# Output stores moved from GpSimd's queue to SyncE's queue in a forward-and-backward joint-network kernel

## The chip, the cores and the metric

The kernel runs on one core of a Trainium2 chip. Its engines are TensorE (PE, with its weight loads shown apart as PEld), VectorE (DVE), ScalarE (ACT), GpSimd (POOL) and SyncE (SP). The transfers between memory and the on-chip buffers are made by 16 DMA engines, which all issuing engines share. The metric is device time of the core in microseconds (us), the median of several runs. The profile is one execution, taken by the hardware profiler.

## The reference

The forward pass takes x (2 batches, 16000 steps, 256 channels). A convolution of width 3 with weights w1 is followed by gelu and by dropping every second step; the same again with w2. The 4000 steps that remain in each batch go through w_f and are joined with each of 8 label rows of g (through w_g) by a sum and a tanh; w_o gives the output, 2 x 4000 x 8 x 256. Then the gradients of all seven inputs are formed from grad_out, which has the output's shape. All data are bfloat16.

```python
def _fwd_reference(x, w1, w2, g, w_f, w_g, w_o):
    h = zeros;  for i in range(3): h = h + einsum("btc,cd->btd", xp[:, i:i+T, :], w1[i])
    h = _gelu(h)[:, ::2, :]
    f = zeros;  for i in range(3): f = f + einsum("btc,cd->btd", hp[:, i:i+T1, :], w2[i])
    f = _gelu(f)[:, ::2, :]
    fe = jnp.einsum("btd,de->bte", f, w_f)
    ge = jnp.einsum("bud,de->bue", g, w_g)
    j = jnp.tanh(fe[:, :, None, :] + ge[:, None, :, :])
    return jnp.einsum("btud,dv->btuv", j, w_o)

_out, _vjp = jax.vjp(_f, x, w1, w2, g, w_f, w_g, w_o)
_grads = _vjp(grad_out)
```

## The kernel before

**Tiling.** The 4000 remaining steps of a batch are cut into nine chunks: one of 256, seven of 512 and one of 160 in the first batch; seven of 512, one of 256 and one of 160 in the second. That makes 18 chunks. The loop at the end of the kernel (lines 973 to 1000) goes over them as a software pipeline. While chunk k is in its joint stage (`stage_j`), the forward convolutions of chunk k+1 (`stage_a`) and the backward pass of chunk k-1 (`stage_de`) run in between.

**What is moved, and by whom.** SP issues:

- XC (x transposed, one buffer of this class) for the convolutions, from `load_xc`;
- GOT (grad_out transposed, 8 buffers), one transfer per chunk and label, from `load_got`;
- GO_R (grad_out in rows, 6 buffers), 2 labels by up to 256 steps, from `load_gor`;
- X5 (x in rows, 4 buffers), one transfer per block of 128 steps, from `load_x5`;
- HRo, HRs, HRe and FR (rows of the activations, made by transposing transfers from one on-chip tile to another), from `dma_rows`;
- at the end, the weight gradients out of the g_sq tiles (two buffers).

POOL issues the two large outputs: out (OUT_SB, 6 buffers, stored in `stage_j`, lines 676 to 688) and the gradient of x (GX_SB, 3 buffers, stored in `stage_de`, lines 841 to 853). A pair of labels and half a chunk (256 steps) fill one OUT_SB; PE's results are copied into it by ACT or DVE (line 674), two blocks of 128 steps one after the other. A block of 128 steps of the gradient of x fills one GX_SB. POOL also copies the one-column halos between chunks and clears pads.

**First and last blocks.** At the first block of a batch the first of its four phases falls outside of x, so that X5 and GX_SB are moved as 1 row and then 127 rows; at the batch's last block a few rows are left. All other blocks are moved with 128 rows.

**What sets the order.** Nothing is issued as the code is read. Every operation is recorded by `F.op` with an estimated cost, its reads and writes, the buffers it opens and a due time. Then `Flow.issue` (lines 104 to 191) runs through a model of the machine: at each step it takes the operation that can start first, among equals the one due first, and writes it to its engine's instruction list. So a change in the model's times changes the order of all lists. Each engine then executes its list in order, and waits for the semaphores of what it depends on. The lines of the model that matter here:

```python
if o.work:                                   # a transfer (line 128)
    ln = lanes[e == "POOL"]
    if len(ln) >= 8:
        s = max(s, ln[-8] + wake)
...
o.done = ring[e] + 2000.0 + self.MARGIN      # line 174; MARGIN is 6500 ns
lanes[e == "POOL"].append(o.done - 1.0 * self.MARGIN)
```

A transfer is believed complete at `done`, and a buffer that it reads is believed free from then. The list `lanes` holds when recent transfers are believed to be over, apart for POOL and for the others: a transfer may not start before the eighth before it in the same list. In the model a store on POOL costs 750 ns of issue for out and 550 for the gradient of x, a plain transfer on SP 400 and a transposing one 1260 (line 332). In the built program eight semaphores in turn serve the transfers of SP and another eight those of POOL, and each transfer waits for the one that had its semaphore before.

Of the kernel before, what the change touches and what calls it, by code (L numbers as in the profile page):

```python
# [17 lines left out]
GELU_A = float(2.0 * np.sqrt(2.0 / np.pi))  # L18


LOADQ, STOREQ = "SP", "POOL"
HR_AT = (0.7, 0.4, 0.3)
A_AT = (0.1, 0.25, 0.4, 0.6)

# [16 lines left out]
class Flow:  # L41
# [62 lines left out]
    def issue(self):  # L104
        T = {e: 0.0 for e in self.WAKE}
        avail = {e: [] for e in T}
        ring = {"SP": 0.0, "POOL": 0.0, "ACT": 0.0}
        lanes = {True: [], False: []}
        left, prog = len(self.ops), -1e12
        slots, seq = self.slots, self.seq  # L110

        def put(o):
            o.ready = max((d.done for d in o.deps), default=0.0)
            for e in o.eng:
                avail[e].append(o)

        for o in self.ops:
            if o.left == 0:
                put(o)
        while left:  # L120
            best = None
            for e, lst in avail.items():
                t, wake, cand = T[e], self.WAKE[e], None
                for o in lst:
                    if o.nb is not None and prog < o.nb:
                        continue
                    s = o.ready + wake
                    if o.work:
# [3 lines that stand above are left out]
                    for b in o.new:  # L132
                        st = seq[b.cls]
                        if not st[2] and st[1] != b.seq:
                            s = None
                            break
                        f = min((x[1] for x in slots[b.cls] if x[1] is not None), default=None)
                        if f is None:
                            s = None
                            break  # L140
                        s = max(s, f + wake)
                    if s is None:
                        continue
                    k = (max(s, t), o.prio, o, e)
                    if cand is None or k < cand:
                        cand = k
                if cand is not None and (best is None or cand[0] < best[0]):
                    best = cand
            if best is None:
                prog = min((o.nb for lst in avail.values() for o in lst if o.nb is not None and o.nb > prog), default=None)  # L150
                assert prog is not None, "no operation can start"
                continue
            s, _, o, e = best
            if o.lead:
                prog = max(prog, o.prio[0])
            for x in o.eng:
                avail[x].remove(o)
            for b in o.new:
                free = [i for i, x in enumerate(slots[b.cls]) if x[1] is not None]
                i = min(free, key=lambda i: (slots[b.cls][i][1], i))  # L160
                b.slot, slots[b.cls][i][1] = i, None
                seq[b.cls][1] += 1
                b.t = slots[b.cls][i][0].tile(b.shape, b.dtype, name=b.name, tag=b.cls)
            T[e] = s + o.cost[o.eng.index(e)]
            if o.work:
                a = max(ring[e], T[e] - 400.0)
                if e == "POOL":
                    ring[e] = a + o.work
                    for q in ("SP", "ACT"):
                        if ring[q] > a:  # L170
                            ring[q] += o.work
                else:
                    ring[e] = max(a, ring["POOL"]) + o.work
                o.done = ring[e] + 2000.0 + self.MARGIN
                lanes[e == "POOL"].append(o.done - 1.0 * self.MARGIN)
            else:
                o.done = T[e] + self.TAIL[e]
            o.inst = o.fn(e)
            for h in o.hold:
                self.tc.add_manual_dep(o.inst.ins, h.inst.ins.name, mybir.DependencyInfo(  # L180
                    mybir.DependencyClass.Sync, mybir.DependencyReason.DATA), reason="order of the first loads")
            left -= 1
            for b in o.bufs:
                b.users -= 1
                if b.users == 0 and b.cls is not None:
                    slots[b.cls][b.slot][1] = o.done
            for d in o.succ:
                d.left -= 1
                if d.left == 0:
                    put(d)  # L190
        self.T = T
# [838 lines left out]
```

## Time and profile before

| | |
|---|---|
| median of 3 runs | 841.24 us (841.03 to 841.38) |
| profiled execution | 841.38 us |
| span of the profiled execution | 839.6 us |
| PE busy | 803.0 us, 96% |
| DVE, ACT busy | 763.0 us, 749.2 us |
| POOL busy | 185.3 us, 22% |
| POOL's stores of out, issue | 136 (95.5 us) |
| POOL's stores of the gradient of x | 68, median 0.56 us each |
| DMA queue of SP (q1) | 120.54 MB, 71.0% of 16 engines |
| DMA queue of POOL (q0) | 49.98 MB, 18.9% of 16 engines |

A row of a timeline gives the start in us from the span's start, the duration, the engine, the line, the operation and its tiles. "SPq" is SP's issuing of a transfer; the duration is that of issuing, with any wait inside it, and the landing of the data comes later. "X" in the profile is X5, "XC" the transposed x; buffer numbers are left out. A DMA view gives the bytes moved in 40 equal slices of its window, in GB/s, and then the transfers issued in the window with the median time from issue to landing, where it could be matched.

### The profile page before, as it was taken

How to read it: one execution, taken by the hardware profiler on the slowest of the kernel's cores; microseconds unless marked ns; L12 is line 12 of the kernel's file. 1: busy time of each engine (PE TensorE's matmuls, PEld its weight loads, DVE VectorE, ACT ScalarE, POOL GpSimd, SP SyncE). 2: the span in 40 equal slices, each digit the busy share in tenths (PEclk: the TensorE clock that was granted, in tenths of full speed). 3: DMA queues.
4: the chain of work that ended last, by engine and by line, in shares of the span. 5: the costliest groups of instructions: out<-in, count | busy, mean ns of one | idle time of the engine just before them, and what ended most of it. 6: DMA issues, size and time to landing. Idle time of an engine off the chain costs nothing.

```text
span 839.6 us, 18037 instructions
## 1 busy us (share of the span) xinstructions
PE 803.0 (96%) x6428; PEld 595.5 (71%) x6428; DVE 763.0 (91%) x1731; ACT 749.2 (89%) x1206; POOL 185.3 (22%) x391
## 2 busy tenths in 40 slices
PE   7479999999999999999999999999999999999994
PEld 5346767677686767877777677676776868788983
DVE  4679999998999989998989999998989999998992
ACT  5859999999899998988899999998898989988762
POOL 2101221212122111223131303121121212123241
PEclk9889999999999999999999999999999999999998
DMA  9989999999989896987988999999899896958442
GB/s 181 128 158 237 198 224 240 262 244 228 226 207 241 200 254 153 219 224 196 187 189 118 245 223 264 241 209 267 220 222 229 212 247 166 255 154 200 125 138 67
DMA packets 330594, 172.06 MB, mean 205 GB/s; under 512 B 275142, under 2 KB 310250, under 8 KB 330504
## 3 DMA queue, kind: packets, MB, share of 16 engines
q1 hardware_dynamic: 313944, 120.54, 71.0%
q0 software_dynamic: 15776, 49.98, 18.9%
q8 instruction: 50, 0.82, 0.4%
q10 hardware_dynamic: 784, 0.39, 0.2%
q14 instruction: 40, 0.33, 0.1%
HBM read 54.44 MB, written 50.34 MB: 125 GB/s over the span
## 4 chain that ended last, share of the span: by engine, by line
PE 72%; DVE 11%; ACT 7%; DMA 3%; issue 3%; SPq 2%; POOL 0%; DVEq 0%; ACTq 0%; POOLq 0%
PE ps L306 58%; PE GWO L306 10%; PE psb L483 4%; SPq L329 2%; DVE NGZ L651 2%; DVE ZS L659 2%; DMA GOT<-in_grad_out_dram 2%; ACT g_sq L432 1%; DVE g_s L436 1%; ACT JT L589 1%; ACT JR L609 1%; ACT JSQ L641 1%; ACT OUT_SB L314 1%; DVE JR L602 1%; DMA out_dram<-g_sq 1%
## 5 line engine op out<-in xcount | busy, mean ns | idle before, releaser
L589 ACT ACTIVATE JT<-FE,GE 128x512 bf16<-128x512 bf16 (+2 forms) x288 | 187.7, 689 | 0.7 <-DVE FE L319 0.7
L331 POOL DMA_DIRECT2D out_dram<-OUT_SB x136 | 95.5, 702 | 361.8 <-ACT OUT_SB L314 242.0
L306 PE MATMUL ps<-GOT,WT 128*128 128x512 bf16 (+2 forms) x576 | 154.8, 354 | 13.1 <-DMA GOT<-in_grad_out_dram 12.8
L651 DVE SCALAR_TENSOR_TENSOR NGZ<-JSQ,ps 128x512 f32<-128x512 bf16 (+2 forms) x252 | 152.1, 606 | 14.6 <-PE ps L306 14.5
L306 PE MATMUL ps<-WO,JT 128*128 128x256 bf16 x1024 | 153.9, 273 | 1.6 <-ACT JT L589 1.0
L609 ACT ACTIVATE JR<-JR 128x1024 bf16<-128x1024 bf16 x128 | 138.2, 1085 | 4.2 <-DVE JR L602 3.9
L641 ACT ACTIVATE JSQ<-JT 128x1024 bf16<-128x1024 bf16 (+2 forms) x119 | 117.5, 990 | 24.1 <-DVE NGZ L651 24.0
L306 PEld LDWEIGHTS <-JT 128*128 128x128 bf16 x1024 | 99.6, 98 | 54.8 <-ACT JT L589 1.8
L306 PE MATMUL GWO<-GO_R,JR 128*128 128x256 bf16 x1024 | 133.6, 274 | 1.1 <-ACT JR L609 1.1
L314 ACT CAST OUT_SB<-ps 128x512 bf16<-128x512 f32 x205 | 125.5, 613 | 9.6 <-PE ps L306 9.6
L659 DVE TENSOR_TENSOR ZS<-ZS,NGZ 128x512 f32<-128x512 f32 (+2 forms) x216 | 131.1, 610 | 0.2
L306 PEld LDWEIGHTS <-WT 128*128 128x128 bf16 x864 | 81.7, 98 | 49.1 <-DMA GOT<-in_grad_out_dram 13.1
L306 PEld LDWEIGHTS <-JR 128*128 128x128 bf16 x1028 | 100.3, 98 | 19.9 <-ACT JR L609 2.7
L306 PEld LDWEIGHTS <-W 128*128 128x128 bf16 x648 | 61.8, 99 | 58.0 <-issue 3.7
L306 PE MATMUL ps<-XC,W 128*128 128x512 bf16 (+2 forms) x432 | 93.5, 355 | 0.8 <-DVE NGZ L651 0.8
L306 PE MATMUL ps<-ROWS,X 128*128 128x256 bf16 x768 | 92.0, 273 | 0.0
L602 DVE TENSOR_TENSOR JR<-FER,GEB 128x1024 bf16<-128x1024 bf16 x128 | 87.2, 683 | 1.0 <-PE GWO L306 1.0
L306 PEld LDWEIGHTS <-X 128*128 128x128 bf16 x768 | 75.1, 98 | 9.1
L436 DVE SCALAR_TENSOR_TENSOR g_s<-g_sq,ps 128x512 bf16<-128x512 bf16 (+2 forms) x108 | 65.9, 611 | 15.8 <-ACT HTo L434 12.6
L707 DVE TENSOR_TENSOR ACC<-ACC,ps 128x512 f32<-128x512 f32 x96 | 64.1, 678 | 11.5 <-PE ps L306 11.3
L432 ACT ACTIVATE g_sq<-ps 128x512 bf16<-128x512 f32 (+2 forms) x108 | 60.4, 559 | 15.3 <-PE ps L306 12.7
L306 PE MATMUL ps<-WT,GHe 128*128 128x256 bf16 x384 | 73.3, 273 | 0.7 <-ACT ROWS L314 0.7
(135 smaller groups left out, 1264.0 us busy)
## 6 DMA issues: line engine op xcount, KB each, us to landing
GO_R<-in_grad_out_dram SPq DMA_DIRECT2D x120, 256.0 KB, 3.9
out_dram<-OUT_SB POOLq DMA_DIRECT2D x120, 256.0 KB, 4.4
X<-in_x_dram SPq DMA_DIRECT2D x60, 320.0 KB, 5.5
out_dram<-GX_SB POOLq DMA_DIRECT2D x60, 256.0 KB, 4.1
GOT<-in_grad_out_dram SPq DMA_TRANSPOSE x144, 4.7
out_dram<-g_sq SPq DMA_DIRECT2D x9, 128.0 KB, 1.8
GO_R<-in_grad_out_dram SPq DMA_DIRECT2D x8, 128.0 KB, 3.1
out_dram<-OUT_SB POOLq DMA_DIRECT2D x8, 128.0 KB, 3.2
```

The costliest lines, as they stand in the source:

```text
L306: nc.tensor.matmul(ps_ap, lhsT=lhsT, rhs=rhs, start=start, stop=stop)
L314: nc.scalar.copy(out=dst(), in_=src())
L331: return eng_.dma_start(out=out(), in_=in_())
L432: op("ACT", c_act(W, True), lambda e, mt=mt, ps=ps: nc.scalar.activation(out=sq[:, mt, :W], in_=ps[:, :W], func=ACT.Square, scale=GELU_SQR ...
L436: op("DVE", c_dve(W), lambda e, mt=mt, ps=ps: nc.vector.scalar_tensor_tensor(out=s[:, mt, :W], in0=sq[:, mt, :W], scalar=1.0, in1=ps[:, :W ...
L589: op("ACT", c_act(W, ptr=True), lambda e, j=j, mt=mt: nc.scalar.activation(out=JT[:, j, mt, :W], in_=S["FE"][:, mt, :W], func=ACT.Tanh, bi ...
L602: op("DVE", c_dve(n * 2 * D, 0.5), lambda e, lo=lo, n=n, m=m, JR=JR: nc.vector.tensor_tensor(out=JR[:m, lo % 2:lo % 2 + n], in0=S["FER"][: ...
L609: op("ACT", c_act(n * 2 * D), lambda e, lo=lo, n=n, m=m, JR=JR: nc.scalar.activation(out=JR[:m, lo % 2:lo % 2 + n], in_=JR[:m, lo % 2:lo % ...
L641: nc.scalar.activation(out=JSQ[:, :, :W], in_=JT[:, j, :, :W], func=ACT.Square)
L651: op("DVE", c_dve(W) + 6, lambda e, d2=d2, ps=ps, u=u, zap=zap, JSQ=JSQ: nc.vector.scalar_tensor_tensor(out=zap(), in0=JSQ[:, d2, :W], sca ...
L659: op("DVE", c_dve(W), lambda e, d2=d2, dst=dst, NGZ=NGZ: nc.vector.tensor_tensor(out=dst[:, d2, :W], in0=ZS[:, d2, :W], in1=NGZ[:, :W], op ...
L707: op("DVE", c_dve(512), lambda e: nc.vector.tensor_tensor(out=acc_ap().rearrange("p k d -> p (k d)"), in0=acc_ap().rearrange("p k d -> p ( ...
```

## The change

The queue of the steady stores becomes SP in place of POOL. All transfers in the steady state are then issued by SP, in one list. And in the planner's model of the limit of eight transfers in flight, a transfer is believed over 0.6 x 6.5 us = 3.9 us before its believed completion, in place of 6.5 us.

```diff
-LOADQ, STOREQ = "SP", "POOL"
+LOADQ, STOREQ = "SP", "SP"
...
                 o.done = ring[e] + 2000.0 + self.MARGIN
-                lanes[e == "POOL"].append(o.done - 1.0 * self.MARGIN)
+                lanes[e == "POOL"].append(o.done - 0.6 * self.MARGIN)
```

A store on SP costs 400 ns of issue in the model (line 332). The stores that use `STOREQ` are those of out and of the gradient of x, 204 in number; the small outputs at the end and the loads of the weights stay where they were.

## The prediction

> **What bounds the kernel now.** I read the page's busy shares first, then busy time by stretch of the span, then the stage in which the changed queue has least room.
>
> The page, section 1, and the slices of section 2:
>
> ```profile
> PE 803.0 (96%) x6428; PEld 595.5 (71%) x6428; DVE 763.0 (91%) x1731; ACT 749.2 (89%) x1206; POOL 185.3 (22%) x391
> ...
> PE   7479999999999999999999999999999999999994
> ```
>
> Busy time in three stretches; the columns are PE, PEld, DVE, ACT, POOL, granted clock, DMA share, GB/s:
>
> ```profile
> 0.00:63.00 63.00, 42.17 (x287) 27.22 (x287) 37.25 (x112) 39.48 (x74) 10.24 (x28) 0.86 0.91 156
> 63.00:798.00 735.00, 730.75 (x5847) 542.54 (x5848) 701.04 (x1542) 691.65 (x1097) 162.82 (x335) 1.00 0.94 215
> 798.00:839.60 41.60, 30.03 (x297) 25.69 (x294) 24.69 (x79) 18.09 (x37) 12.24 (x28) 0.95 0.33 104
> ```
>
> TensorE is the bound. From 63 to 798 us it idles 735.0 - 730.8 = 4.2 us at the full clock, so nothing there can be gained, and any wait that reaches PE is added to the end. The start loses 20.8 us and the end 11.6. The question is whether the reordered SP queue can keep PE's inputs and, above all, the output buffers coming.
>
> How the trace prices a transfer over 127 rows: load_x5 has two such loads (the first block of each batch), on SP already. SP's own issue rows, then the DMA view of 439 to 455 us (40 slices of 0.4 us):
>
> ```profile
> 437.41 1.96 SPq L331 DMA_DIRECT2D X<-in_x_dram  x5
> 439.47 14.71 SPq L329 DMA_TRANSPOSE GOT<-in_grad_out_dram  x1
> 454.27 0.53 SPq L331 DMA_DIRECT2D GO_R<-in_grad_out_dram  x1
> ```
>
> ```profile
> GB/s 436 182 192 155 183 239 312 284 191 70 29 26 26 26 26 26 323 333 36 26 26 26 51 155 193 35 19 26 26 26 26 26 26 29 27 23 26 26 26 26
> ...
> X<-in_x_dram SPq DMA_DIRECT2D x1, 317.5 KB
> ```
>
> After the 317.5 KB load the core moves 26 GB/s, a tenth of its usual rate: one DMA engine works and 15 rest, for 325,120 B / 26 GB/s = 12.5 us. SP's next transpose takes 14.7 us to issue instead of the median 1.28. The same load sits in the start: 26 GB/s from 34 to 42 us, and PE's longest wait (12.8 us, for GOT) ends behind it.
>
> The store with the same 127 rows is on POOL today, and lands like any other:
>
> ```profile
> out_dram<-GX_SB POOLq DMA_DIRECT2D x1, 254.0 KB, 3.6
> ```
>
> Who needs the queue at that time: POOL issued that store at 95, SP was issuing without a pause up to 124, and ACT's copy into the 15th output buffer came at 118.7:
>
> ```profile
> 95.17 1.07 POOL L331 DMA_DIRECT2D out_dram<-GX_SB  x2 [1.32 <-ACT GX_SB L316]
> ```
>
> ```profile
> 116.60 2.55 SPq L329 DMA_TRANSPOSE FR<-FT  x2
> 119.24 0.53 SPq L331 DMA_DIRECT2D GO_R<-in_grad_out_dram  x1
> 119.83 4.02 SPq L329 DMA_TRANSPOSE GOT<-in_grad_out_dram  x3
> ```
>
> ```profile
> 118.69 0.67 ACT L314 CAST OUT_SB<-ps 128x512 bf16<-128x512 f32 x1
> ```
>
> **What the skill says.** The Trainium skill, "DMA: Bandwidth & Descriptors", section "Why a DMA increments its semaphore by 16 and not by 1": a hardware-generated transfer is spread over the largest k up to 16 that divides the slowest dimensions, so 127 partitions go to one engine, the lowest-numbered, while the software path from POOL uses 16 engines for 127. The trace agrees on both: 26 GB/s for the load on SP, 3.6 us to landing for the 254 KB store on POOL. Same page, "Queues, rings and completion order": each engine consumes a queue's ring in order and takes turns between queues. So a 16-way transfer behind a 127-row one in SP's ring has one sixteenth of itself waiting; the 14.7 us row fits. Same page, "SWDGE vs HWDGE vs iDMA": DVE can lock POOL out while it writes descriptors in SBUF, and the hardware path is free of that. No row shows that lockout costing PE anything.
>
> **The change part by part.** Removed: 204 of POOL's steady stores (136 of OUT_SB, mean 702 ns, 95.5 us; 68 of GX_SB, 0.56 us, 38 us). Worth 0: POOL is 22% busy and none of PE's longer waits names it.
>
> Added: the same 204 on SP. Priced as its loads of the same shape (GO_R 0.53, X 0.44 us): 136 x 0.53 + 68 x 0.44 = 102 us. SP now issues some 144 x 1.28 + 144 x 1.25 + 32 x 3.1 + 136 x 0.53 + 68 x 0.44 = 565 us; it gets 667, 79% of the span. Hidden in steady state behind SP's waits for slots (223 us on PE at the transposes alone). Behind each store in SP's order stand the loads, which now wait for its copy by ACT or DVE. GOT (8 buffers) and GO_R (6) are fetched tens of us ahead, so a few us cost nothing. In the built program each SP transfer also waits for the eighth before it; stores now share these eight with loads. At 738 transfers per 840 us and 4 to 5 us to landing, four or five are in flight: binds only behind a long one.
>
> Planner line 175: believed completions in the eight-transfer limit come 0.4 x 6.5 us later. No instruction is added; the order moves. PE's list is identical for 288 matmuls, which is up to 63 us, then permuted. GX_SB's slots are planned with the same distance as before. 0, -1 to +3.
>
> Start: POOL's output stores of 32.4 and 35.9 us took 10.5 us to land, beside the 127-row load. They now come after PE's long wait: two sixteenths of 256 KB leave that engine, 2 x 16 KB / 26 GB/s = 1.2 us. Estimate -1 (0 to -2.5).
>
> First 127-row store (GX_SB of the first chunk). Its issue: before, SP issues 41 transfers from 63.7 to 119.8. In the new order the store comes after the same list without one GOT (1.3), one GO_R (0.6) and two X (1.6), with eight stores at 0.6, and one store earlier (0.6): 56.1 - 3.5 + 4.8 + 0.6 = 58.0, so at 121.7, less 1 from the start: 120.7. It moves 260,096 B at 26 GB/s, 10.0 us, and some 3 us of fixed landing time (3.6 minus 0.6 transfer on POOL): 133.7. Directly behind it stands the store of the 9th output buffer: 134. With six buffers the 15th takes the slot of the 9th, and ACT's copy into it waits for this landing. ACT gets there at 118.7 - 1 = 117.7, and stands 16 us, with tanh, squares and PSUM copies queued behind it. PE goes on until its seven PSUM banks are full, at 0.43 us for two 512-column matmuls some 2 to 3 us. Cost 14 us (9 to 20; below if it issues earlier, above if the next stores, held by SP's blocked transpose, come late too).
>
> Second 127-row store (first chunk of batch two): POOL issued it at 508.4, and the fourth GX_SB block, which takes its slot, was copied at 520.3. From SP at 509 or later it lands at 522: 2 us late, more by SP's backlog (up to 10). Take +3 (0 to 12). Tail: the output chain (g_sq stores, 1.85 us each) stays on SP; the last GX_SB stores are ready before it: 0, +-1.
>
> Sum: -1 + 14 + 3 + 1 (scattered late slots) = +17. The profiled execution is 841.38 us, 1.78 around its span of 839.6; the median of the runs is 841.24, 0.14 less. So span 856.6, time 858.4, for the median 858.
>
> **Rivals.** (1) The store spreads over 16 engines from SP too, or the buffers absorb it. For: PE has been full through the SP hold-up of 439 to 454. Against: the slot is needed 16 us before landing. Then only the eight extra issues count: the store of the 7th buffer issues near 102 and lands at 106.6, against a copy at 106.1. +2 to +6: 845. (2) SP becomes the bound. For: its transposes took 1.25 to 2.4 us each between 85 and 104, with a DMA share of 1.04. At 1.7 each, 288 x 0.45 = 130 us more: 667 + 130 + two holds of 13 = 823 of 840, and late slots recur in every chunk: +35 to +60, 885. Against: 1.25 us is common from 110 on. (3) Faster: the start gains its 1 to 2.5 us and both 127-row stores hide: 839.5. It decides if the first issues before about 105, so that it lands by 118.7. For that SP would have to shed 16 us of its list; against, it is continuously issuing there. (4) No change: a loss of 1 in slots against the start, 841.
>
> **How the numbers follow.** Main case 0.66, its own range 850 to 872 (parts: start -2.5 to 0, first store 9 to 20, second 0 to 12). Rival 1: 0.13; 2: 0.10; 3: 0.06; 4: 0.05. The range 842 to 880 leaves rivals 3 and 4 (0.11) below, and most of 2 (0.08) above. A difference under 0.2% (1.7 us) can't be told from none: faster 0.06, same 0.05, slower 0.89.
>
> **What would show it.** Right: 26 GB/s for some 10 us from about 121, an SP transpose issue over 8 us there, ACT idle before an OUT_SB copy on DMA, PE idle 9 to 20 us in one gap between 115 and 140, a small one near 520, and 4 us elsewhere. PE's first 63 us shorter by 1. Wrong: GX_SB's 254 KB store landing in 4 to 5 us from SP; PE gaps spread evenly over chunks (SP the bound); a PE busy time that itself grew.

## The result and the profile after

The changed kernel takes 870.3 us (median of 6 runs, 868.11 to 872.49) against 841.31 us of the kernel before beside it (6 runs): a ratio of 1.034, 95% interval 1.0317 to 1.0362, or 29.0 us more. The profiled execution has a span of 866.9 us, 27.3 more than before.

The page of the changed kernel, busy shares and the slices of PE and of its clock:

```profile
PE 809.1 (93%) x6428; PEld 597.5 (69%) x6428; DVE 763.2 (88%) x1733; ACT 747.7 (86%) x1204; POOL 57.1 (7%) x187
...
PE   8489959999999999999999996799999999999994
...
PEclk9799989999999999999999999899999999999998
```

POOL is freed of 128 us of work, and nobody gains by it. PE has the same 6428 matmuls, is busy 6.1 us longer, and shows two new dents: a 5 in the sixth slice (108 to 130 us), and a 6 and a 7 from 520 to 563 us, each time with a lower clock.

Busy time in the same three stretches as before (stretch, length, then PE, PEld, DVE, ACT, POOL, granted clock, DMA share, GB/s):

```profile
0.00:63.00 63.00, 45.61 (x309) 30.02 (x310) 40.29 (x119) 42.22 (x78) 7.27 (x24) 0.89 0.82 151
63.00:800.00 737.00, 708.24 (x5579) 519.33 (x5578) 673.34 (x1459) 668.44 (x1055) 41.92 (x140) 0.99 0.93 209
800.00:867.00 67.00, 55.26 (x544) 48.20 (x542) 49.56 (x157) 37.01 (x73) 7.92 (x23) 0.95 0.42 128
```

In the middle PE idled 4.2 us before; now it idles 737.0 - 708.2 = 28.8 us. The start lost 3.4 us of idling (17.4 for 20.8). The end is as it was (11.7 for 11.6).

PE's waits, costliest first (total us, times, longest us):

```profile
PE ps L306 <- ACT ROWS L314: 12.2, 3, 10.5
PE ps L306 <- ACT GX_SB L316: 11.9, 2, 11.2
PE ps L306 <- DMA GOT<-in_grad_out_dram: 10.5, 1, 10.5
```

The third is the start's wait, 12.8 us before. The first two are new, and each is one long gap. The span's growth thus adds up: -3.4 (start) + 10.5 (first gap) + 11.2 (second) + 2.8 (the rest of the middle: 24.5 - 21.7) + 0.1 (end) + 6.1 (PE busy longer) = 27.3 us.

**The first gap.** The chain that ended last, 113 to 135 us:

```profile
113.92 12.62 DMA out_dram<-OUT_SB
126.62 0.35 ACT OUT_SB L314
...
127.11 1.03 ACT ROWS L314
128.17 6.41 PE ps L306 x28
```

SP's issues there, and the bytes moved from 100 to 140 us (40 slices of 1 us):

```profile
113.14 0.68 SPq L331 DMA_DIRECT2D out_dram<-GX_SB  x2
113.92 3.26 SPq L331 DMA_DIRECT2D out_dram<-OUT_SB  x1
117.23 5.93 SPq L329 DMA_TRANSPOSE GOT<-in_grad_out_dram  x1
```

```profile
GB/s 170 311 369 288 231 10 130 131 58 296 144 89 69 132 8 14 20 82 159 168 68 25 27 25 27 25 186 312 378 295 377 302 245 293 6 273 380 305 412 368
```

The store of 127 rows goes out at 113.5 as the second of the pair; its data had been copied by 91.5. Directly behind it stands a full-width store of out, which lands 12.6 us after its own issue; only then may ACT copy into that buffer. The five slices at 25 to 27 GB/s from 121 to 126 us fit the one-engine store alone on the queue: from 121.2 to 125.8 us the 16 DMA engines are busy 0.07 of the time, and one of 16 is 0.0625.

**The second gap** has the same face, with the buffer of the gradient of x itself (chain, then SP):

```profile
532.11 13.13 DMA out_dram<-GX_SB
545.35 0.60 ACT GX_SB L316
```

```profile
531.78 4.70 SPq L331 DMA_DIRECT2D out_dram<-GX_SB  x3
536.58 4.14 SPq L329 DMA_TRANSPOSE GOT<-in_grad_out_dram  x1
```

The data of that store was ready much earlier. A GX_SB block takes two copies; ACT's first begins at 516.72 and the second ends near 519.2. The store is issued at 532, nearly 13 us later. (POOL, before, issued it 1.2 us after its second copy.)

**PE's clock after a gap.** Stretches of 4 us (length, PE busy, granted clock, DMA share, GB/s):

```profile
126.00:130.00 4.00, 1.83 (x9) 0.50 1.05 293
130.00:134.00 4.00, 4.00 (x20) 0.63 1.57 304
134.00:138.00 4.00, 4.00 (x29) 1.00 0.87 241
545.00:549.00 4.00, 3.00 (x8) 0.50 1.13 181
549.00:553.00 4.00, 4.00 (x25) 0.95 0.94 158
```

After the first gap PE comes back at half its clock at 128.2 us: its first eight 256-column matmuls take 1.86 us, where eight such take 1.04 before the gap. If the clock is either half or whole, a mean of 0.63 means half speed for 3.0 of the 4 us, so the slow spell lasts about 5 us. After the second gap, from 546.0, it lasts about 3.4 us by the same reckoning. The Trainium skill, "TensorE: Matmul & The Clock Gate", section "Part 1: The HAM clock gate (the "warmup" mystery)", gives the array these two rates: an idle window of some 3.4 us drops it to half, and about 3.4 us of sustained work releases it. The trace agrees after the second gap; after the first the slow spell is longer.

Half speed takes 0.50 x 1.83 + 0.37 x 4.00 = 2.4 us from PE after the first gap and 0.50 x 3.00 + 0.05 x 4.00 = 1.7 us after the second. That is at most 4.1 of the 6.1 us by which PE is busy longer; where the rest comes from was not found.

### The profile page after: what moved, and what is told of

It is laid out like the page before. It is cut to its first block, busy times and chain, and to the rows that moved or that the text cites. A ratio compares the mean times of both kernels' runs of the same rounds, so it can differ in the third digit from the quotient of the medians.

```text
span 866.9 us, 17921 instructions
## 1 busy us (share of the span) xinstructions
PE 809.1 (93%) x6428; PEld 597.5 (69%) x6428; DVE 763.2 (88%) x1733; ACT 747.7 (86%) x1204; POOL 57.1 (7%) x187
## 4 chain that ended last, share of the span: by engine, by line
PE 64%; DVE 13%; ACT 13%; DMA 6%; issue 2%; SPq 0%; DVEq 0%; ACTq 0%; POOL 0%
PE ps L306 52%; PE GWO L306 9%; PE psb L483 3%; ACT JT L589 3%; DVE NGZ L651 2%; ACT JR L609 2%; DVE g_s L436 2%; DVE ZS L659 2%; DMA out_dram<-GX_SB 2%; ACT g_sq L432 1%; DMA out_dram<-OUT_SB 1%; DMA GOT<-in_grad_out_dram 1%; ACT OUT_SB L314 1%; ACT JSQ L641 1%; DVE GHo L763 1%
## 5 line engine op out<-in xcount | busy, mean ns | idle before, releaser
L306 PE MATMUL ps<-GOT,WT 128*128 128x512 bf16 (+2 forms) x576 | 154.8, 355 | 11.0 <-DMA GOT<-in_grad_out_dram 10.5
L641 ACT ACTIVATE JSQ<-JT 128x1024 bf16<-128x1024 bf16 (+2 forms) x115 | 113.7, 992 | 23.3 <-DVE NGZ L651 22.7
L306 PE MATMUL ps<-XC,W 128*128 128x512 bf16 (+2 forms) x432 | 94.9, 359 | 12.0 <-ACT GX_SB L316 11.2
L436 DVE SCALAR_TENSOR_TENSOR g_s<-g_sq,ps 128x512 bf16<-128x512 bf16 (+2 forms) x108 | 66.0, 611 | 23.8 <-ACT HTo L434 17.4
L306 PE MATMUL ps<-WT,GHo 128*128 128x256 bf16 x384 | 73.1, 273 | 0.7 <-ACT GX_SB L316 0.7
L432 ACT ACTIVATE g_sq<-ps 128x512 bf16<-128x512 f32 (+2 forms) x108 | 60.0, 555 | 14.5 <-PE ps L306 11.5
```

The source lines that it names most:

```text
L306: nc.tensor.matmul(ps_ap, lhsT=lhsT, rhs=rhs, start=start, stop=stop)
L432: op("ACT", c_act(W, True), lambda e, mt=mt, ps=ps: nc.scalar.activation(out=sq[:, mt, :W], in_=ps[:, :W], func=ACT.Square, scale=GELU_SQR ...
L436: op("DVE", c_dve(W), lambda e, mt=mt, ps=ps: nc.vector.scalar_tensor_tensor(out=s[:, mt, :W], in0=sq[:, mt, :W], scalar=1.0, in1=ps[:, :W ...
L641: nc.scalar.activation(out=JSQ[:, :, :W], in_=JT[:, j, :, :W], func=ACT.Square)
```

## The experiments

Differences are medians against the kernel before of the same group of runs: 842.61 us for the first four, 841.51 for the next four, 841.66 for the last three. On that footing the change costs +29.0 us. Most of them use one of two small edits, which leave the planner's order as it is. The first sends a transfer to another issuer than the planner's:

```diff
-            eng_ = nc.sync if e == "SP" else nc.gpsimd if e == "POOL" else nc.scalar
+            eng_ = nc.sync if (via or e) == "SP" else nc.gpsimd if (via or e) == "POOL" else nc.scalar
```

The second issues a transfer in two pieces, where its rows are 127:

```diff
-                return eng_.dma_start(out=out(), in_=in_())
+                return [eng_.dma_start(out=out()[lo:hi] if hi else out(), in_=in_()[lo:hi] if hi else in_()) for lo, hi in cuts][-1]
```

### The two 127-row stores, both and one by one

The kernel after; of the 204 moved stores, the two with 127 rows are issued by POOL again.

```diff
-                    bytes_=(r1 - r0) * 2048, cost=550.0)
+                    bytes_=(r1 - r0) * 2048, cost=550.0, via="POOL" if r1 - r0 == 127 else None)
```

> The changed kernel with its two 127-row stores of the gradient of x, alone, back on POOL; every engine's list is otherwise the same, and the other 202 stores stay on SP. Theory A (each 127-row store from SP runs on one DMA engine and holds the slots and the ring behind it): both PE gaps (10.5 us near 117 to 128, 11.2 us near 534 to 546) and the slow clock after them (PE busy 6 us longer) go: 839 to 843 us, PE busy near 803, 254 KB store landing in 4 to 6 us. Theory B (SP's longer list and the smaller packets of its queue cost it): the loss stays spread, 860 to 870 us.

Measured: 854.39 us, ratio 1.0141 (1.0113 to 1.0169), +11.8 us, between the two forecasts. Two stores out of 204 carry 17 of the 29 us; the rest is not explained by them. PE's busy time fell to 806.8 us and not to 803, so that part of its growth does not hang on the two stores either. Then only the first batch's, and only the second's (`and b == 0`, `and b == 1` in the condition):

> As the run before, but only the first batch's 127-row store goes back to POOL. Theory A: the gap near 117 to 128 goes with its slow clock, the one near 534 stays: 13 to 14 us less than the changed kernel, 855 to 858 us. Theory B: within 2 us of 870.

Measured: 863.2 us, 1.0248 (1.0216 to 1.0281), +20.6.

> Only the second batch's 127-row store goes back to POOL. Theory A: the gap near 534 to 546 goes with its slow clock, the first stays: 14 to 16 us less than the changed kernel, 854 to 857 us; with the run before the two savings add up to that of both. Theory B: within 2 us of 870.

Measured: 859.93 us, 1.0207 (1.0187 to 1.0228), +17.3. Both fell above what was expected, as the first run had. Each store has its own gap: with the first on POOL, PE idles 0.7 us from 100 to 150 and 16.0 from 520 to 560; with the second on POOL 11.3 and 2.0. With only the first store moved, PE's idling in the second stretch grew from 11.9 us to 16.0, which fits that run's saving less than was forecast. The savings, 8.4 and 11.7, sum to 20.1 against 17.2 for both. But something else still takes 12 us. With both on POOL one wait of ACT shows where:

```profile
ACT GX_SB L316 <- DMA out_dram<-GX_SB: 9.7, 2, 7.4
```

The buffers of the gradient of x still come free late, with no slow store among them.

### One engine or the queue: cutting the store

In the kernel after, the two stores stay on SP, each as 112 and then 15 rows.

```diff
-                    bytes_=(r1 - r0) * 2048, cost=550.0)
+                    bytes_=(r1 - r0) * 2048, cost=550.0, cuts=((0, 112), (112, 127)) if r1 - r0 == 127 else ((0, None),))
```

> The changed kernel with all stores on SP, each 127-row store cut into one of 112 and one of 15 rows. Theory A: what hurts is that all rows go to one engine, not the queue: as with both on POOL, 839 to 844 us, no stretch at 26 GB/s near 115 or 532. Theory B, or the order of SP's list as cause: 860 to 872 us, since SP gets two more transfers.

Measured: 853.75 us, 1.0119 (1.0098 to 1.014), +11.1, again between the two forecasts and the same as on POOL within the noise. Neither gap is left at its size; PE was busy 39.15 and 28.06 us in these two stretches of the kernel after:

```profile
100.00:150.00 50.00, 47.67 (x369) 34.17 (x368) 47.48 (x100) 47.55 (x74) 1.42 (x4) 1.00 0.99 217
520.00:560.00 40.00, 36.40 (x255) 24.07 (x253) 30.83 (x64) 31.15 (x49) 2.53 (x8) 1.00 1.02 238
```

So for these two stores SP's queue is no worse than POOL's; what hurts is that 127 rows go out in one piece. SP's rows of this run show a candidate for a part of the remaining 11 us:

```profile
462.98 6.99 SPq L331 DMA_DIRECT2D X<-in_x_dram  x3
470.06 6.93 SPq L329 DMA_TRANSPOSE GOT<-in_grad_out_dram  x1
```

That is the 127-row load of x in the second batch: the same shape, on SP in both kernels. Before, no store of the two outputs stood behind it in SP's list. Now they do: the first GX_SB block of the second batch is copied by 514.4 and its store is issued at 528.2.

### The two parts of the diff apart

The constant alone (0.6 in line 175, the stores on POOL), and the queue alone (the stores on SP, the constant 1.0):

```diff
-                lanes[e == "POOL"].append(o.done - 1.0 * self.MARGIN)
+                lanes[e == "POOL"].append(o.done - 0.6 * self.MARGIN)
```

```diff
-LOADQ, STOREQ = "SP", "POOL"
+LOADQ, STOREQ = "SP", "SP"
```

> The planner's constant alone (0.6 in place of 1.0), stores on POOL as before. If the order that the constant gives is harmless: within 2 us of 841. If the new order of PE's and SP's lists itself costs: above 845.

> The queue alone (stores on SP), the planner's constant at 1.0 as before. Theory A: both one-engine stores are there, so the loss stays, 855 to 880 us, moved with the place that the planner gives the two stores in SP's list. If the constant made the loss: near 841.

Measured: 841.09 us for the constant, 0.9997 (0.9988 to 1.0005); 869.05 us for the queue, 1.0333 (1.0316 to 1.035), +27.5. Within the noise the queue makes the whole loss.

### The two stores alone, in the kernel before

The kernel before, in which only the two 127-row stores go to SP (`via="SP" if r1 - r0 == 127 else None`); all others stay on POOL.

> The kernel before, with its two 127-row stores alone on SP; all other stores stay on POOL and all other lists are the same. Theory A in full (a one-engine store costs only through the slot behind it that is needed before it lands): the first is issued near 106 and no output store stands behind it in SP's ring, so it costs nothing; the second is issued near 510, lands 13 us later and holds the fourth gradient block, copied at 520: 3 to 6 us. 842 to 848. A rival (a one-engine store costs by holding SP, wherever it stands): two gaps of about 10 us, above 858.

Measured: 852.04 us, 1.0117 (1.0097 to 1.0137), +10.5, between what the theories gave. The two stores differ. The first holds SP for 11.5 us in one row, and costs nothing (SP's rows, then the stretch from 100 to 150 us: length, PE busy, clock, DMA share, GB/s):

```profile
108.48 0.39 SPq L331 DMA_DIRECT2D out_dram<-GX_SB  x1
108.92 11.47 SPq L329 DMA_TRANSPOSE HRo<-HTo  x2
```

```profile
100.00:150.00 50.00, 49.66 (x384) 1.00 1.08 198
```

The stores of out are not behind it here, they are on POOL. So the first gap of the kernel after is not SP's stop as such, but the buffers of out whose stores stand in the stopped ring. The second store does cost: PE waits 6.3 us for a copy of GX_SB, since the fourth block needs the slot of the slow store itself, and from 520 to 560 us it idles 7.6 us where it idled 0.3 before. Its clock averages 0.87 there, which the forecast of 3 to 6 us had left out.

### Four buffers for the gradient of x

The kernel after, with one buffer moved from GO_R to GX_SB:

```diff
-                    ("fer", 2), ("gsq", 2), ("gs", 2), ("jt", 3), ("got", 8), ("go", 6), ("out", 6), ("rows", 3), ("hte", 2), ("jr", 3),
+                    ("fer", 2), ("gsq", 2), ("gs", 2), ("jt", 3), ("got", 8), ("go", 5), ("out", 6), ("rows", 3), ("hte", 2), ("jr", 3),
...
-                    ("gf", 1), ("gfh", 2), ("ngfe", 1), ("x5", 4), ("gx", 3), ("ghh", 2)):
+                    ("gf", 1), ("gfh", 2), ("ngfe", 1), ("x5", 4), ("gx", 4), ("ghh", 2)):
```

> The kernel after with four buffers for grad x instead of three (and five for grad_out rows instead of six, to make room). Theory A: the second gap comes from the fourth block taking the slot of the first, whose store is slow; with a fourth buffer TensorE does not wait for it, the gap of about 11 us near 540 shrinks to 0 to 4 us, and the time falls to 858 to 864. The first gap, which hangs on the buffers of out, stays. Rival B: the full ring also stops SyncE's transposes, so that TensorE waits for grad_out instead: 866 to 872.

Measured: 857.29 us, 1.0174 (1.0127 to 1.022), +15.6, just under the range of A. The second gap is gone, though the slow store is issued as late as before (SP's row, then the stretch from 520 to 560 us with the columns as above; with three buffers PE was busy 28.06 us of it):

```profile
533.31 4.74 SPq L331 DMA_DIRECT2D out_dram<-GX_SB  x3
```

```profile
520.00:560.00 40.00, 39.53 (x289) 1.00 0.92 172
```

So SP's transposes behind the store do not hold PE; the slot does. The lost GO_R buffer has its own price elsewhere (4.1 us of waits for GO_R).

### Cutting the loads

First the kernel before, its two 127-row loads of x cut into 112 and 15 rows, nothing else:

```diff
-                r=[], w=[(X5, "m")], bytes_=(r1 - r0) * 2560, new=new, at=at, hold=hold, cost=550.0)
+                r=[], w=[(X5, "m")], bytes_=(r1 - r0) * 2560, new=new, at=at, hold=hold, cost=550.0, cuts=((0, 112), (112, 127)) if r1 - r0 == 127 else ((0, None),))
```

> The kernel before, with its two 127-row loads of x cut into 112 and 15 rows. PE's longest wait at the start (12.8 us, for GOT) stands behind the first of them. If the one-engine load is its cause: that wait falls to 3 us or less, 830 to 835 us, faster than both kernels. If GOT is late for another reason (its slot, the eight transfers in flight): within 2 us of 841.

Measured: 828.25 us, 0.984 (0.9826 to 0.9855), 13.3 us less than before, more than was expected. It is the fastest kernel of this study. The start's 12.8 us wait for GOT is gone:

```profile
0.00:63.00 63.00, 52.50 (x383) 35.17 (x384) 49.60 (x140) 51.99 (x95) 13.55 (x33) 0.97 0.91 194
```

PE is busy 52.5 us of the first 63, for 42.2, and its clock there is 0.97 for 0.86. Then the same cut in the kernel after, with the stores left whole:

> The kernel after, with only the 127-row loads of x cut, and the stores left whole on SyncE. Theory A: 13 us at the start are gained as in the kernel before (841.5 to 828.2), and the two store gaps stay, the second somewhat smaller because SyncE's list is not already late from the load: 852 to 858. Rival B: the stores are late for SyncE's list alone and the load has no part in it: just the start's 13 us go, 857 to 859, and the gap in the second batch stays at 11 us.

Measured: 849.81 us, 1.0094 (1.0069 to 1.0119), +8.2: 20.8 us better than the kernel after, 7.5 more than the cut brought to the kernel before, and some 2 us under the range. By place, PE's idling falls by 6.4 us in the first 63 us (17.4 to 11.0; in the kernel before the cut took off 10.3 there) and by 6.2 us from 520 to 560 us (11.9 to 5.8). So the second batch gains here what it had no need to gain in the kernel before (SP's rows, 454 to 545 us):

```profile
458.64 2.73 SPq L331 DMA_DIRECT2D X<-in_x_dram  x4
461.46 1.31 SPq L329 DMA_TRANSPOSE GOT<-in_grad_out_dram  x1
...
512.64 4.52 SPq L331 DMA_DIRECT2D out_dram<-GX_SB  x3
```

The load no longer stops SP, and the store follows its data by 6 us (copied by 506.7) where it was 13. ACT's wait for that slot falls from 14.8 to 7.7 us, PE's from 11.2 to 4.1. In the kernel after the same load and the transpose behind it took SP 13.3 us (6.39 from 468.06, 6.93 from 474.56), for 4.0 here; of these 9 us, 7 were still there at 531, after 50 us of list. The other 6 of the 13 us by which the store was late are there without the slow load too.

Last, both kinds cut:

> The kernel after, with both the 127-row stores of grad x and the 127-row loads of x cut into 112 and 15 rows; all on SyncE. Theory A: what is left of the loss once the stores are cut (about 12 us against the kernel before) is the one-engine load of x in batch two, which keeps SyncE for some 14 us near 465 with the stores behind it; with it cut too, moving the stores costs next to nothing against the kernel before with cut loads (828.2): 828 to 834. Rival B: SyncE's longer list and the ring shared by loads and stores cost about 12 us by themselves, whichever engines the bytes use; then 838 to 842.

Measured: 834.1 us, 0.9904 (0.9882 to 0.9926), 7.6 us less than before, at the edge of A's range and below B's. PE's longest waits are small:

```profile
PE ps L306 <- ACT ROWS L314: 4.4, 3, 2.6
PE ps L306 <- DMA W<-in_w_dram: 2.6, 1, 2.6
PE ps L306 <- DMA GOT<-in_grad_out_dram: 2.5, 1, 2.5
```

All in one table, us against the kernel before of the same runs:

| | stores on POOL | stores on SP, 127 rows cut | stores on SP, whole |
|---|---|---|---|
| loads of 127 rows whole | 0 | +11.1 | +29.0 |
| loads cut | -13.3 | -7.6 | +8.2 |

Read along the rows: the stores' move costs 29.0 us with whole loads and 21.5 with cut ones, but 5.7 when no transfer with 127 rows is left on SP. One-engine stores make 16 to 18 us of the change's loss and the one-engine loads some 5 to 8 more beyond what they cost the kernel before; for that of the second batch the lateness of the stores behind it is seen. About 6 us remain.

These 6 are not settled by a run, but the last trace shows most of them in one place. Directly behind the stores of the first gradient blocks SP issues a store of out at 105.86 us, and it lands 2.7 us later; ACT has waited 3.2 us for it, PE idles 2.6 us, less than the skill's window of 3.4, and still runs at half its clock from about 111 to 114. That is the first gap in small, with no slow transfer in front of it: the store is late for its place in SP's list. ACT also waits 3.2 us for one store of the gradient of x.

## Why the prediction was right, and where it was not

The time, 870.3, lies in the range and inside the likeliest case's own range (850 to 872), near its upper end; the sum was +17 and came out as +27 in the profiled execution. The mechanism was the forecast one, but the sizes were not: the second gap came out 8 us larger than its term, PE's longer busy time added 6 that stood in no term, and the first gap and the start were 6 us better than theirs. That errors of this size cancelled in part and left the time inside the range is partly luck. Step by step:

- **PE is the bound, a late buffer is paid in full.** Right. The middle's 4.2 us of idling became 28.8, and all of it is in the span.
- **Start, -1.** Right in sign, under-sized: the wait for GOT is 10.5 for 12.8, and 3.4 us of idling are gone in all. Single executions differ by some 2 us there (23.1 us of idling in the run with the constant alone, for 20.8 before), and no run isolates the cause that was given.
- **204 stores on SP, hidden in its waits.** Right in the main: SP's waits for PE at its transposes fell from 223.5 to 138.0 us, by most of the 102 us that were added. The two late places are the exception.
- **First store, +14 (9 to 20).** Right in mechanism at each link, as the chain shows: one engine, the store of out directly behind it, ACT's copy, PSUM's cushion. The store of out behind it landed 13.0 us after the slow store's issue (10 + 3 was reckoned) and PE ran on 2.1 us after ACT stopped (2 to 3). What was off is the issue time, 113.5 for 120.7: 2.7 us since SP got through the first chunk 3.7 us earlier and not 1, the rest since SP's list from there on took 53.5 us where the sum of rows gave 58.0. One of the eight stores of out in that sum had gone out earlier, at 47.3, and some rows of before had run longer than the same transfers did after (a pair of XC transposes 6.35 us, later 2.37 + 2.62; two GOT 4.71, later 1.24 + 1.47): they were taken as costs, and fit waits. ACT stood 11.0 us and not 16; the gap was 10.5.
- **Second store, +3 (0 to 12).** This is the term that failed. Landing 13 us after issue was right (13.1), the fourth block's need for the slot too (more buffers remove the gap). But the issue was put at 509, right behind the data, and the store came nearly 13 us after its data, since SP was late: 7 us of that go when the 127-row load of the second batch is cut, and 6 stay. The text had named SP's backlog "(up to 10)" and put it in the bound, not in the value. The gap was 11.2 us.
- **PE at half its clock after a gap.** Not in the sum at all. PE's busy time grew by 6.1 us, which the prediction listed as a sign that would speak against it. That sign did not speak against the gaps: the matmuls are the same 6428, and the slow spells right after the two gaps give 2.4 + 1.7 us, so a gap of 11 us in PE cost about 2 us more than its length. The rest stays open: in the two runs in which these gaps are gone or small (stores back on POOL, stores cut) PE is still busy 806.8 and 806.4 us for 803.0 before.
- **Scattered, +1; planner's constant, 0; tail, 0.** 2.8, nothing (0.9997), 0.1.
- **Rival 2, SP as the bound with late slots in every chunk.** Wrong as put: there are two gaps, not many. But it holds a part of the truth: SP had little slack in the second batch, where of a stop of 9 us 7 were left some 50 us later, and that is how the load's stop reached the stores. Rival 1 fell with the 25 to 27 GB/s; 3 and 4 with the time.
- **The load of the first batch as a cost of its own.** The prediction saw 26 GB/s and PE's longest wait behind it, and used both only as a price for the store. Cutting the two loads was worth 13.3 us in the kernel before, and PE's idling fell almost only in the start (20.8 to 10.5 us in the first 63).

## What to carry to other kernels

Before moving transfers onto a hardware queue, look through its list for shapes that go to one DMA engine (127 rows here): here each held the ring for 10 us and more, and what came later in that ring was late; it cost most where a store's buffer was needed soon. Cutting such a transfer into 112 and 15 rows is a small edit. For the loads alone it gave 13.3 us, while the move still cost 5.7 us when everything was cut. A list with little slack carries a stop on for tens of us, so price a late store by the place where its queue really is, not by when its data is ready, and add the slow clock to a long PE gap (here about 2 us for one of 11 us).

## What the runs showed of the hardware

- The same bytes make more packets from SP. The queues' lines on the page after, whose counterparts before were 313944 packets and 120.54 MB for SP and 15776 packets and 49.98 MB for POOL:

```profile
q1 hardware_dynamic: 357120, 169.71, 87.1%
...
q0 software_dynamic: 384, 0.81, 0.4%
```

  The 49.17 MB of stores take 43176 packets on SP and took 15392 on POOL, yet the time of the engines in the two queues is much the same: 87.5% of 866.9 us, 759 us, for 89.9% of 839.6 us, 755 us.
- A whole 317.5 KB load of 127 rows in the start costs PE 12.8 us of waiting and a clock of 0.86 in the first 63 us; in 112 and 15 rows it costs neither (0.97).
- A stop in SP's ring did no harm to PE where only transfers fetched well ahead stood behind it (11.47 us in one row, PE 49.66 of 50 us busy). At the start, where the loads behind it were needed at once, PE waited 12.8 us. Where a store whose buffer was needed landed some 13 us after its issue, PE idled 10.5 and 11.2 us.
